# A fused attention and mixer kernel: the weight conversion's shift as a ScalarE copy, softmax sums inverted by groups of query tiles

## The chip, the cores and the metric

The kernel runs on one core of a Trainium2 chip. The metric is the device time of one execution in microseconds. Three runs of the kernel before took 928.18, 929.75 and 927.37 us; their median is 928.18. In what follows PE is TensorE, DVE is VectorE, ACT is ScalarE, POOL is GpSimd and SP is SyncE. PEld is PE's weight load, and a name with a q at its end is an engine's own queue or sequencer.

## The reference, cut to what matters

Three stages run in a row, for 4 batches of 576 tokens. Attention has 8 heads of 64 columns, is causal and has a bias from a running sum of `s`; a gated feed-forward part (512 to 1024 to 512) and a token and channel mixer (256 and 1536 wide) follow. The part that the change touches in the first stage is the softmax:

```python
scores = np.where(causal, -1000000000.0, scores + np.minimum(bias, 0.0))
scores = scores - np.max(scores, axis=-1, keepdims=True)
attn = np.exp(scores)
attn = attn / (np.sum(attn, axis=-1, keepdims=True) + 1e-09)
return np.matmul(attn, v).astype(np.float32)
```

The weights of the two later stages arrive as float64: they are drawn as float32 and multiplied by a float64 scalar.

## The kernel before, in words

**Tiles and stages.** A head's 576 query rows are cut into five tiles j = 0 to 4 of 128 rows, the last of 64. Causality leaves tile j the first 128 j + 128 (or 576) keys. Tiles 0 and 1 make up a head's first chunk (256 columns, `QC`), tiles 2 to 4 its second (320, `CM`). Batch 0 is done in float32: `early` (L300) does tiles 0 and 1 of its 8 heads, `late` (L346) tiles 2 to 4. Batches 1 to 3 are 24 visits, one for each head, with operands split into a high and a low part: `scores` (L265), `transposes` (L387) and `values` (L425).

**One query tile.** PE writes the scores to PSUM. DVE adds the mask, writes the negated scores to the SBUF tile P and keeps the row's extremum (`softmax_max`, L247). `softmax` (L256) then has ACT take the exponential in place, with the row sum as a second output (L260), DVE add 1e-9 (L261) and invert (L262), and POOL multiply P by the inverse (L263). PE transposes P by 128 columns (L314, L365 or L397), ACT copies the transposed tile from PSUM (for batches 1 to 3 with the difference to it from DVE, L422 and L423), and PE multiplies it with the values (L324, L383, L445). P has one buffer for each j (in `early` two), the transposed tile has two PSUM banks.

**Weights.** They come in 85 pieces. `weight_load` (L537) brings a piece as pairs of 32-bit words, and `weight_split` (L546) makes float32 of them: ACT multiplies the high words (L549), DVE shifts the low words right by 29 bits in place (L550), DVE joins three bits and the rest of the high words (L551), then the sign (L552); for one matrix ACT halves the result (L554). ACT writes the high part (L555), and POOL, or DVE for that matrix, the low part (L556). 12 pieces are 512 words wide, 69 are 256 and 4 are 288. The first 12 (`w_k`, `w_r`) and the 16 of `w_v` are converted beside batch 0's attention, the others (`w_tok1`, `w_ch1`, `w_tok2`, `w_ch2`) after attention has ended, beside the feed-forward part of the last batch and the start of the mixer. Raw pieces use 5 buffers at first, later 6.

**The order of the work.** The program is unrolled. Each instruction belongs to one engine, and each engine works in the order of its own queue. That order is made when the program is built: a planner plays the program through with its own costs for each instruction and takes, among those whose inputs it holds ready, the one of highest priority. `at(place)` (L67) sets the priority. Attention items stand at places 16 + n, three to a head for batch 0, five for a visit; feed-forward units of a batch stand behind the items that they are to run beside, so that PE has products between the steps of softmax. `attention_item` (L580) emits an item, with the loads and splits of later heads. `place` (L234) issues four transfers and `load` (L203) one, all on SP's queue, where the weights' loads are issued too.

**What depends on what around the change.** A tile's transposes need its P normalised. P's buffer comes free for the next head after the transposes. The feed-forward part needs on POOL the low part of the squares (L475, tile KK), in the same queue as the normalisations and the weights' low parts.

Of the kernel before, what the change touches and what calls it, by code (L numbers as in the profile page):

```python
# [8 lines left out]
F32 = mybir.dt.float32  # L9
F32R = mybir.dt.float32r  # L10
BF16 = mybir.dt.bfloat16
I32 = mybir.dt.int32
AF = mybir.ActivationFunctionType
ALU = mybir.AluOpType
# [9 lines left out]
def attention_moe_mixer(  # L24
# [16 lines left out]
    nc = tc.nc  # L41
    G, D, _, S = qk.shape
# [10 lines left out]
    NS = (S + 127) // 128  # L53
    QC = 256
# [3 lines left out]
    scale = 1.0 / float(D) ** 0.5  # L58
# [21 lines left out]
    const = ctx.enter_context(tc.tile_pool(name="const", bufs=1, reuse_waits="tile"))  # L80
# [5 lines left out]
    ident = const.tile([128, 128], F32, name="ident")  # L86
# [36 lines left out]

    # P^T of the first chunk: key block 0, then what causality leaves of key block 1. Of the
    # second chunk: key block k at BLK[k], the last in columns that its neighbour leaves unused.
    FIRST = QC + 128
    BLK = [CM * k for k in range(NS - 1)] + [CM * (NS - 2) - (128 * (NS - 1) - QC)]
    ft, pt = {}, {}

    # Tiles that batch 0 uses in float32 and the rest as float32r parts.  # L130
    def x_tile(slot, dtype=F32):
        return qk_p.tile([128, 2 * S], dtype, tag=f"X{slot}", name=f"X{slot}").rearrange("p (t s) -> p t s", t=2)

    def pt_tile(slot, dtype=F32):
        return pt_p.tile([128, (NS - 1) * CM], dtype, tag=f"PT{slot}", name=f"PT{slot}")
# [20 lines left out]

    # Rows (1, -8 cum_q) and (8 cum_k, 1) whose products add the bias, in float32 for the
    # first chunk of batch 0 and as hi and lo for the rest.
    def bias_rows(cp):
# [34 lines left out]

    # A visit is a head and the query tiles it covers. Per pair of heads HL holds
    # (q_lo, q_hi, k_lo, k_hi); per head X1 holds (q, k) as [bias rows; zeros; hi] and
    # X2 holds [q_lo; q_hi] and [k_hi; k_lo].
    HLv = HL.rearrange("p (t s) -> p t s", t=4)
# [48 lines left out]
    def softmax_max(j, ps, P, mx, x, c0, c1):  # L247
# [6 lines left out]
        )  # L254

    def softmax(j, P, mx, x):  # L256
        m = min(128, S - 128 * j)
        w = 128 * j + m
        sm = st_p.tile([128, 2], F32, tag="sum", name="sum")
        nc.scalar.activation(out=P[0:m, 0:w], in_=P[0:m, 0:w], func=AF.Exp, bias=mx[0:m, x:x + 1], scale=-1.0, accum_out=sm[0:m, 0:1])  # L260
        nc.vector.tensor_scalar(out=sm[0:m, 0:1], in0=sm[0:m, 0:1], scalar1=1e-9, scalar2=1.0, op0=ALU.add, op1=ALU.mult)  # L261
        nc.vector.reciprocal(out=sm[0:m, 1:2], in_=sm[0:m, 0:1])  # L262
        nc.gpsimd.tensor_scalar(out=P[0:m, 0:w], in0=P[0:m, 0:w], scalar1=sm[0:m, 1:2], scalar2=1.0, op0=ALU.mult, op1=ALU.mult)  # L263

# [15 lines left out]

    # Batch 0's first chunk, in float32 throughout: HL holds (q, k) of four heads, two more
    # tiles of two each.
    early_at = [(HL, 0, 4)]
# [16 lines left out]
    def early(h, j, V0, cp):  # L300
# [8 lines left out]
        if j == 0:  # L309
            pt[0] = ps_t.tile([128, 512], F32, tag="t", name="t")  # L310
        ps = pt[0]
        for k in range(j + 1):
            o = 128 * (j + k)
            nc.tensor.transpose(ps[:, o:o + 128], P[:, 128 * k:128 * k + 128], ident)  # L314
        if j == 0:
            return
        T = cp.tile([128, FIRST], F32, tag="T", name="T", bufs=2)
        copy("A", T, ps[:, 0:FIRST])
# [10 lines left out]

    # Batch 0's second chunk, in float32 too.  # L330
    late_x, late_v, late_t, late_ps = {}, {}, {}, {}
# [14 lines left out]
    def late(h, j):  # L346
        m = min(128, S - 128 * j)
        w = 128 * j + m
        q0 = 128 * j
# [8 lines left out]
        softmax(j, P, mx, y)  # L358
        if j == QC // 128:
            late_t[h] = pt_tile(h % 2)  # L360
        T = late_t[h]
        pt = ps_t.tile([128, 512], F32, tag="t", name="t")
# [115 lines left out]

    # sigmoid(z) = (tanh(z / 2) + 1) / 2; the half is in w_v.
    def gate(b, c, m):  # L480
# [62 lines left out]

    # float64 words to float32 bits (scaled by 2 ** -half), then to two 12-bit parts: 2 ** -112
    # on the high word, read as a float32, is the change of exponent bias.
    def weight_split(key, hi, lo, half=0):  # L546
        t = raw.pop(key)
        low, high = t[:, :, :, 0], t[:, :, :, 1]
        copy("A", f32(high), f32(high), 2.0 ** -112)  # L549
        nc.vector.tensor_scalar(out=low, in0=low, scalar1=29, scalar2=None, op0=ALU.logical_shift_right)  # L550
        nc.vector.scalar_tensor_tensor(out=low, in0=high, scalar=3, in1=low, op0=ALU.logical_shift_left, op1=ALU.bitwise_or)  # L551
        nc.vector.scalar_tensor_tensor(out=low, in0=high, scalar=-2 ** 31, in1=low, op0=ALU.bitwise_and, op1=ALU.bitwise_or)  # L552
        if half:
            copy("A", f32(low), f32(low), 0.5)  # L554
        copy("A", hi, f32(low))  # L555
        (nc.vector if half else nc.gpsimd).tensor_tensor(out=lo, in0=f32(low), in1=f32(hi), op=ALU.subtract)  # L556
# [23 lines left out]
    def attention_item(n):  # L580
# [48 lines left out]
        with at(N0 + n):  # L629
            scores(i, j)  # L630
            transposes(i, j)
        with at(N0 + n + 0.3):
# [132 lines left out]

    # The low part of the last rows of YN lies below their high part, to meet the high part
    # of w_tok1 (in both halves) in one pass with it.
    def y_transpose(b, h):
# [151 lines left out]
```

## Time and profile before

The profiled execution has a span of 925.0 us from its first to its last instruction. The page gives the span alone, so no other time of that execution is known; it lies 3.2 us under the median of the three runs.

| | us of busy time | share of the span | instructions |
|---|---|---|---|
| PE | 877.3 | 95% | 6032 |
| PEld | 801.9 | 87% | 6032 |
| DVE | 542.4 | 59% | 1667 |
| ACT | 444.4 | 48% | 1211 |
| POOL | 297.6 | 32% | 405 |
| span of the profiled execution | 925.0 | | 17127 |
| median of three runs | 928.18 | | |

Busy time is the union of an engine's instructions, waiting left out. Matmuls are pipelined, so a busy PE is not a PE at its peak. The shares are means over stages that differ: up to some 75 us batch 0's attention and the first weights, up to 450 us attention and feed-forward together, up to 600 us the rest of the feed-forward part with the mixer's weights, then the mixer alone.

### The profile page before, as it was taken

The page shows a single profiled execution, that of the slowest core. Times are in us where ns is not written, and L with a number is a line of the kernel's source. Part 1 is how long each engine was busy: PE and PEld are TensorE (multiplying, and loading weights), DVE is VectorE, ACT ScalarE, POOL GpSimd, SP SyncE. Part 2 cuts the span into 40 slices and gives each one's busy share as a digit, 9 for nine tenths or more (in the row PEclk, how much of TensorE's full clock was granted, in tenths as well). Part 3 has the DMA queues.
Part 4 walks back from the last instruction along what each step waited for, and adds up shares of the span by engine and source line. Part 5 has one row for each costly group of instructions (what it writes and reads, how often), then busy time and mean ns, then how long its engine had stood idle before and what let it go on. Part 6 is the DMA issues. An engine that isn't in the chain of part 4 may idle for free.

```text
span 925.0 us, 17127 instructions
## 1 busy us (share of the span) xinstructions
PE 877.3 (95%) x6032; PEld 801.9 (87%) x6032; DVE 542.4 (59%) x1667; ACT 444.4 (48%) x1211; POOL 297.6 (32%) x405
## 2 busy tenths in 40 slices
PE   6869999999899999899999688999999999999998
PEld 4427678998799999899999578999999999999998
DVE  6897776677798567886479967632223222322220
ACT  4667757767777756668376645321112111311120
POOL 5673446644665625554154644200000000000000
PEclk9988999999899999899999899999999999999999
DMA  7952445455643535442125543500010001000000
GB/s 180 267 130 73 121 92 129 108 134 136 143 97 97 116 82 132 94 110 40 52 83 161 160 141 119 181 7 15 15 44 12 15 16 43 12 9 22 18 6 29
DMA packets 57222, 79.61 MB, mean 86 GB/s; under 512 B 6144, under 2 KB 36096, under 8 KB 57136
## 3 DMA queue, kind: packets, MB, share of 16 engines
q1 hardware_dynamic: 55264, 77.92, 32.4%
q8 instruction: 48, 0.79, 0.3%
q10 hardware_dynamic: 1872, 0.59, 0.3%
q14 instruction: 38, 0.31, 0.1%
HBM read 46.67 MB, written 10.03 MB: 61 GB/s over the span
## 4 chain that ended last, share of the span: by engine, by line
PE 71%; DVE 10%; DMA 8%; issue 5%; ACT 3%; POOL 2%; SPq 0%; ACTq 0%; POOLq 0%; DVEq 0%
PE c L107 32%; PE vd L107 7%; PE h L107 7%; PE t L107 4%; PE pv L445 4%; PE r L107 4%; PE t L397 3%; DMA X<-HL 2%; PE s L275 2%; PE s L276 2%; DVE raw L552 2%; PE pv L383 2%; DVE raw L551 1%; DMA raw<-in_moe_w_ch_dram 1%; DVE t L461 1%
## 5 line engine op out<-in xcount | busy, mean ns | idle before, releaser
L107 PE MATMUL c<-XR,C 128*128 128x320 f32 (+1 forms) x1152 | 158.6, 298 | 2.9 <-DVE KK L780 2.1
L107 PEld LDWEIGHTS c<-XR,C 128*128 128x128 f32 x1152 | 155.2, 190 | 4.2 <-DVE KK L780 3.1
L263 POOL TENSOR_SCALAR P<-P,sum 64x576 f32<-64x576 f32 (+4 forms) x160 | 107.4, 675 | 118.1 <-DVE sum L262 56.1
L107 PE MATMUL vd<-KK,WV 128*128 128x256 f32 (+1 forms) x768 | 124.6, 304 | 5.2 <-POOL KK L475 4.9
L107 PE MATMUL h<-XK,WK 128*128 128x256 f32 (+1 forms) x768 | 123.4, 306 | 5.2 <-ACT XK L462 3.6
L107 PEld LDWEIGHTS h<-XK,WK 128*128 128x128 f32 x768 | 109.6, 195 | 9.5 <-ACT XK L462 5.3
L107 PEld LDWEIGHTS vd<-KK,WV 128*128 128x128 f32 x768 | 108.0, 192 | 10.0 <-POOL KK L475 6.1
L260 ACT ACTIVATE P<-P,mx 64x576 f32<-64x576 f32 (+4 forms) x160 | 95.9, 600 | 33.0 <-DVE mx L250 29.3
L107 PE MATMUL c<-KK,WV 128*128 128x256 f32 (+1 forms) x768 | 106.4, 294 | 0.0
L107 PEld LDWEIGHTS c<-KK,WV 128*128 128x128 f32 x768 | 103.0, 188 | 0.0
L779 ACT ACTIVATE KK<-c 128x256 fp32r<-128x256 f32 (+1 forms) x64 | 26.1, 411 | 146.0 <-PE c L107 146.0
L250 DVE CUSTOM_DVE_ANT_0 P<-s,maskc 64x288 f32<-64x288 f32 (+4 forms) x160 | 75.0, 473 | 22.7 <-PE s L276 8.6
L821 DVE TENSOR_TENSOR u<-c,u 128x256 f32<-128x256 f32 (+1 forms) x32 | 14.7, 458 | 123.2 <-PE c L107 123.2
L74 ACT ACTIVATE raw<-raw 128x256 f32<-128x256 f32 (+2 forms) x101 | 46.7, 468 | 43.6 <-DMA raw<-in_moe_w_ch_dram 18.4
L780 DVE SCALAR_TENSOR_TENSOR KK<-c,KK 128x256 fp32r<-128x256 f32 (+1 forms) x64 | 29.1, 456 | 65.5 <-ACT KK L779 65.5
L107 PE MATMUL r<-XR,WR 128*128 128x320 f32 (+1 forms) x384 | 65.6, 306 | 1.4 <-DVE WK L775 1.4
L475 POOL TENSOR_TENSOR KK<-k,KK 128x256 fp32r<-128x256 f32 (+1 forms) x64 | 54.9, 861 | 28.1 <-ACT k L474 27.0
L107 PEld LDWEIGHTS r<-XR,WR 128*128 128x128 f32 x384 | 55.3, 193 | 3.1 <-DVE WK L775 1.6
L107 PE MATMUL c<-XK,WR 128*128 128x320 f32 (+1 forms) x384 | 55.8, 294 | 0.0
L397 PE MATMUL t<-ident,P 128*128 128x128 f32 (+1 forms) x360 | 53.7, 266 | 2.0 <-DVE sum L261 1.1
L107 PEld LDWEIGHTS c<-XK,WR 128*128 128x128 f32 x384 | 52.4, 188 | 0.0
L423 DVE TENSOR_TENSOR PT<-t,PT 128x384 fp32r<-128x384 f32 (+1 forms) x96 | 44.1, 465 | 13.1 <-ACT PT L422 11.7
(109 smaller groups left out, 1521.0 us busy)
## 6 DMA issues: line engine op xcount, KB each, us to landing
X<-HL SPq DMA_DIRECT2D x72, 288.0 KB
raw<-in_moe_w_ch_dram SPq DMA_DIRECT2D x48, 256.0 KB
HL<-in_qk_dram SPq DMA_DIRECT2D x12, 576.0 KB
yt<-y_d SPq DMA_DIRECT2D x16, 288.0 KB
raw<-in_moe_w_k_dram SPq DMA_DIRECT2D x8, 512.0 KB
raw<-in_moe_w_v_dram SPq DMA_DIRECT2D x16, 256.0 KB
VS<-in_v_dram SPq DMA_DIRECT2D x12, 256.0 KB
y_d<-e SPq DMA_DIRECT2D x16, 160.0 KB
```

The source lines that it names most:

```text
L74: nc.scalar.activation(out=out, in_=in_, func=AF.Copy, scale=scale)
L107: nc.tensor.matmul(ps, a, b, start=first and i == 0, stop=last and i == n - 1)
L250: nc.vector.tensor_tensor_reduce(out=P[0:m, c0:c1], in0=ps[0:m, 0:c1 - c0], in1=maskc[0:m, 512 - q0 + c0:512 - q0 + c1], scale=-scale, sca ...
L260: nc.scalar.activation(out=P[0:m, 0:w], in_=P[0:m, 0:w], func=AF.Exp, bias=mx[0:m, x:x + 1], scale=-1.0, accum_out=sm[0:m, 0:1])
L263: nc.gpsimd.tensor_scalar(out=P[0:m, 0:w], in0=P[0:m, 0:w], scalar1=sm[0:m, 1:2], scalar2=1.0, op0=ALU.mult, op1=ALU.mult)
L275: nc.tensor.matmul(ps[0:m, 0:c1 - c0], x1[:, 0, q0:q0 + m], x1[:, 1, c0:c1], start=True, stop=False)
L397: nc.tensor.transpose(ps[0:r, p0 + m * k:p0 + m * k + m], P[0:m, 128 * k:128 * k + r], ident[0:m, 0:m])
L423: nc.vector.tensor_tensor(out=view(PT[1]), in0=pv, in1=f32(view(PT[0])), op=ALU.subtract)
L445: nc.tensor.matmul(ps[:, o:n], vv[0:r, k, :], pair[t], start=(k == 0 and t == 0), stop=(k == nk - 1 and t == 1),)
L475: nc.gpsimd.tensor_tensor(out=kk[:, 1, m, 0:n], in0=t[:, 0:n], in1=f32(kk[:, 0, m, 0:n]), op=ALU.subtract)
L779: nc.scalar.activation(out=hi, in_=ps, func=AF.Relu)
L780: nc.vector.scalar_tensor_tensor(out=lo, in0=ps, scalar=0.0, in1=f32(hi), op0=ALU.max, op1=ALU.subtract)
```

## The change

In `weight_split` the shift of the low words on DVE becomes an ACT instruction, a copy that reads them as unsigned integers, multiplies by slightly less than 2 to the -29, adds -0.496 and writes unsigned integers. In `softmax` the addition, the inversion and the multiplication by the inverse are taken out; the row sums of a group of query tiles go to neighbouring columns of one small tile (four such tiles, filled with 1 at the start and used in turn). `normalize` does one addition and one inversion for the group and one multiplication for each of its tiles. A group is a head's first chunk (tiles 0 and 1) or its second (tiles 2 to 4). All transposes of a group come after its `normalize`; `late`'s become a function of their own. Comments were taken out as well.

```diff
+    sums = []
+    for x in range(4):
+        t = const.tile([128, 2, NS - QC // 128], F32, name=f"sums{x}")
+        nc.gpsimd.memset(t, 1.0)
+        sums.append(t)
+    open_rows = []
+
     def softmax(j, P, mx, x):
         m = min(128, S - 128 * j)
         w = 128 * j + m
-        sm = st_p.tile([128, 2], F32, tag="sum", name="sum")
-        nc.scalar.activation(out=P[0:m, 0:w], in_=P[0:m, 0:w], func=AF.Exp, bias=mx[0:m, x:x + 1], scale=-1.0, accum_out=sm[0:m, 0:1])
-        nc.vector.tensor_scalar(out=sm[0:m, 0:1], in0=sm[0:m, 0:1], scalar1=1e-9, scalar2=1.0, op0=ALU.add, op1=ALU.mult)
-        nc.vector.reciprocal(out=sm[0:m, 1:2], in_=sm[0:m, 0:1])
-        nc.gpsimd.tensor_scalar(out=P[0:m, 0:w], in0=P[0:m, 0:w], scalar1=sm[0:m, 1:2], scalar2=1.0, op0=ALU.mult, op1=ALU.mult)
+        sm = sums[0]
+        y = len(open_rows)
+        nc.scalar.activation(out=P[0:m, 0:w], in_=P[0:m, 0:w], func=AF.Exp, bias=mx[0:m, x:x + 1], scale=-1.0, accum_out=sm[0:m, 0, y:y + 1])
+        open_rows.append((P, m, w))
+
+    def normalize():
+        sm = sums.pop(0)
+        n = len(open_rows)
+        nc.vector.tensor_scalar(out=sm[:, 0, 0:n], in0=sm[:, 0, 0:n], scalar1=1e-9, scalar2=1.0, op0=ALU.add, op1=ALU.mult)
+        nc.vector.reciprocal(out=sm[:, 1, 0:n], in_=sm[:, 0, 0:n])
+        for y, (P, m, w) in enumerate(open_rows):
+            nc.gpsimd.tensor_scalar(out=P[0:m, 0:w], in0=P[0:m, 0:w], scalar1=sm[0:m, 1, y:y + 1], scalar2=1.0, op0=ALU.mult, op1=ALU.mult)
+        open_rows.clear()
+        sums.append(sm)
...
         softmax(j, P, mx, 0)
         if j == 0:
-            pt[0] = ps_t.tile([128, 512], F32, tag="t", name="t")
-        ps = pt[0]
-        for k in range(j + 1):
-            o = 128 * (j + k)
-            nc.tensor.transpose(ps[:, o:o + 128], P[:, 128 * k:128 * k + 128], ident)
-        if j == 0:
             return
+        rows = [r[0] for r in open_rows]
+        normalize()
+        ps = ps_t.tile([128, 512], F32, tag="t", name="t")
+        for y, R in enumerate(rows):
+            for k in range(y + 1):
+                o = 128 * (y + k)
+                nc.tensor.transpose(ps[:, o:o + 128], R[:, 128 * k:128 * k + 128], ident)
...
         softmax(j, P, mx, y)
-        if j == QC // 128:
+        if j == NS - 1:
+            rows = [r[0] for r in open_rows]
+            normalize()
             late_t[h] = pt_tile(h % 2)
+            for y, R in enumerate(rows):
+                late_transpose(h, QC // 128 + y, R)
+
+    def late_transpose(h, j, P):
+        m = min(128, S - 128 * j)
+        q0 = 128 * j
         T = late_t[h]
...
+    TOP3 = 2.0 ** -29 * (1.0 - 2.0 ** -11)
+
     def weight_split(key, hi, lo, half=0):
         t = raw.pop(key)
         low, high = t[:, :, :, 0], t[:, :, :, 1]
         copy("A", f32(high), f32(high), 2.0 ** -112)
-        nc.vector.tensor_scalar(out=low, in0=low, scalar1=29, scalar2=None, op0=ALU.logical_shift_right)
+        nc.scalar.activation(out=low.bitcast(U32), in_=low.bitcast(U32), func=AF.Copy, scale=TOP3, bias=-0.496)
...
             scores(i, j)
-            transposes(i, j)
+            if j in (QC // 128 - 1, NS - 1):
+                normalize()
+                for y in range(0 if j < QC // 128 else QC // 128, j + 1):
+                    transposes(i, y)
```

## Rows read from the trace of the kernel before

**Rows 1.** Stretches: busy us (count) by engine, granted clock, DMA share, GB/s.

```profile
0.00:50.00 50.00, 40.62 (x110) 22.75 (x111) 37.86 (x137) 29.56 (x76) 29.70 (x53) 1.00 0.91 230
50.00:70.00 20.00, 11.25 (x34) 4.36 (x32) 19.46 (x45) 11.93 (x28) 14.34 (x14) 0.77 0.40 91
...
130.00:450.00 320.00, 309.37 (x2183) 284.81 (x2182) 237.09 (x866) 221.53 (x615) 164.05 (x238) 0.98 0.46 106
...
485.00:530.00 45.00, 37.58 (x248) 35.77 (x247) 43.59 (x89) 29.14 (x81) 25.44 (x29) 0.92 0.51 155
530.00:600.00 70.00, 63.48 (x469) 60.90 (x470) 49.74 (x133) 32.39 (x89) 26.86 (x28) 0.95 0.48 150
600.00:925.00 325.00, 321.69 (x2384) 317.51 (x2381) 86.75 (x202) 58.33 (x150) 0.00 (x0) 1.00 0.06 19
```

**Rows 2.** L550: as a group of one shape, then its shortest, median and longest.

```profile
L550 DVE TENSOR_SCALAR raw<-raw 128x256 int32<-128x256 int32 x69 | 26.2, 381 | 19.0 <-DMA raw<-in_moe_w_ch_dram 9.4 <-DMA raw<-in_moe_w_v_dram 5.8 <-DMA raw<-in_moe_w_tok_dram 1.4
...
L550 DVE TENSOR_SCALAR raw<-raw x85: 269/295/1087, 14.2 to 588.8; 128x256 int32<-128x256 int32 x69, 128x512 int32<-128x512 int32 x12, 128x288 int32<-128x288 int32 x4
```

**Rows 3.** DVE's busy us (count) by L550 alone, in the same stretches.

```profile
0.00:50.00 50.00, 5.50 (x11) 1.00 0.91 230
50.00:70.00 20.00, 2.42 (x5) 0.77 0.40 91
...
485.00:530.00 45.00, 10.10 (x22) 0.92 0.51 155
530.00:600.00 70.00, 9.62 (x28) 0.95 0.48 150
```

**Rows 4.** 485 to 530 us: waits (us, times, longest), then a group of POOL.

```profile
POOL C L556 <- ACT C L74: 12.4, 10, 4.5
ACT C L74 <- DVE raw L552: 10.5, 11, 1.5
...
PE vd L107 <- POOL KK L475: 4.9, 3, 2.1
...
L556 POOL TENSOR_TENSOR C<-raw,C 128x256 fp32r<-128x256 f32 x21 | 18.2, 875 | 18.6 <-ACT C L74 12.4 <-DMA y_d<-e 6.2
```

**Rows 5.** Waits of 50 to 70 us.

```profile
PE s L356 <- DVE mx L250: 4.7, 4, 2.3
```

**Rows 6.** ACT's copies of raw words (count, busy us, mean ns, idle us before).

```profile
L74 ACT ACTIVATE raw<-raw 128x256 f32<-128x256 f32 x85 | 36.8, 438 | 37.6 <-DMA raw<-in_moe_w_ch_dram 18.4 <-DMA raw<-in_moe_w_v_dram 9.0 <-DMA raw<-in_moe_w_tok_dram 6.7
...
L74 ACT ACTIVATE raw<-raw 128x512 f32<-128x512 f32 x12 | 8.1, 673 | 4.2 <-DMA raw<-in_moe_w_k_dram 2.1 <-DMA raw<-in_moe_w_r_dram 2.1
```

**Rows 7.** An inversion, an addition; additions' busy us (count) in 50 to 70.

```profile
L262 DVE RECIPROCAL sum<-sum 128x1 f32<-128x1 f32 x128 | 19.6, 155 | 1.8
...
L261 DVE TENSOR_SCALAR sum<-sum 128x1 f32<-128x1 f32 x128 | 18.3, 145 | 21.4 <-ACT P L260 20.7
...
50.00:70.00 20.00, 0.68 (x5) 0.77 0.40 91
```

**Rows 8.** POOL's fills of small tiles.

```profile
L183 POOL MEMSET e<- 32x192 f32 x12 | 2.7, 267 | 7.5 <-DMA ext_d<-e 7.5
```

**Rows 9.** POOL's normalisation of tiles 3, 4 and 2.

```profile
L263 POOL TENSOR_SCALAR P<-P,sum 128x512 f32<-128x512 f32 x32 | 27.5, 858 | 26.0 <-DVE sum L262 14.0 <-ACT PF L406 3.8 <-ACT PT L422 3.0
...
L263 POOL TENSOR_SCALAR P<-P,sum 64x576 f32<-64x576 f32 x32 | 25.4, 793 | 45.1 <-DVE sum L262 21.9 <-ACT PT L422 6.2 <-ACT PF L406 4.4
...
L263 POOL TENSOR_SCALAR P<-P,sum 128x384 f32<-128x384 f32 x32 | 22.3, 696 | 23.9 <-DVE sum L262 9.3 <-PE t L397 4.9 <-DVE sum L261 2.3
```

**Rows 10.** The longest exponential and the longest maximum.

```profile
L260 ACT ACTIVATE P<-P,mx 64x576 f32<-64x576 f32 x32 | 24.7, 773 | 9.8 <-DVE mx L250 7.8 <-DVE sum L262 1.1 <-POOL P L263 0.5
...
L250 DVE CUSTOM_DVE_ANT_0 P<-s,maskc 128x512 f32<-128x512 f32 x32 | 21.8, 682 | 2.1 <-PE t L365 0.6 <-PE s L276 0.6 <-POOL P L263 0.4
```

**Rows 11.** Second-chunk scores of batch 0: shortest/median/longest ns, first and last start.

```profile
L356 PE MATMUL s<-X x64: 406/488/1062, 35.2 to 131.6; 68*64 68x288 f32 x32, 68*128 68x384 f32 x16, 68*128 68x512 f32 x16
```

**Rows 12.** PE's transposes of batches 1 to 3.

```profile
L397 PE MATMUL t<-ident,P 128*128 128x128 f32 (+1 forms) x360 | 53.7, 266 | 2.0 <-DVE sum L261 1.1
```

More of the change, by code (lines that the diff above doesn't have):

```diff
@@ L12 @@
 I32 = mybir.dt.int32
+U32 = mybir.dt.uint32
 AF = mybir.ActivationFunctionType
```

## The prediction

> **What bounds the kernel now.** I read the busy time by stage first. One stretch after another shows which engine is full [rows 1]. From 600 us on, TensorE (PE) works 321.69 of 325 us, VectorE (DVE) 86.75 and ScalarE (ACT) 58.33: nothing the change touches can move that part except by letting it begin earlier. From 130 to 450 us, the attention of batches 1 to 3, PE works 309.37 of 320 us and DVE 237.09. Two stretches look different. In 50 to 70 us DVE works 19.46 of 20 us and PE 11.25, at a granted clock of 0.77, a mean over its two levels, 1.2 and 2.4 GHz. In 485 to 530 us DVE works 43.59 of 45 us and PE 37.58, at 0.92. There DVE is the limit, and PE loses 8.75 and 7.42 us by idle time alone. Before 50 us the limit is partly the DMA engines, at 0.91 of their time, with DVE at 37.86 of 50.
>
> The groups of instructions then show what DVE does in these two stretches: the weights. Each piece of float64 weights takes three DVE instructions (L550 to L552), and the shift L550 takes 381 ns on 256 columns, from 269 to 1087 [rows 2]. By stage it takes 5.50 us before 50, 2.42 in 50 to 70, 10.10 in 485 to 530 and 9.62 in 530 to 600 [rows 3]. The waits of 485 to 530 show how that reaches PE: ACT waits 10.5 us for DVE's raw words, POOL 12.4 us for ACT's high part, and behind those low parts in POOL's queue stands the square's low part (KK, L475), for which PE waits 4.9 us [rows 4]. In 50 to 70 PE waits 4.7 us for DVE's maxima, which free the score banks [rows 5].
>
> **The change, part by part.** *The shift leaves DVE.* 85 instructions go: 69, 12 and 4 by width. DVE loses 5.50, 2.42, 10.10 and 9.62 us in the stages above; the few left over lie where PE is full, at no gain. *ACT gets 85 copies instead.* The trace has no ACT instruction on integers. Its nearest rows are ACT's copies of the neighbouring words, with the same stride and width: 438 ns on 256 columns, 673 on 512 [rows 6]. I take these, since only the type differs. I bound it from below by L550's own quickest run, 269 ns [rows 2], and from above by POOL's 875 ns for the low part of such a piece [rows 4].
>
> In 485 to 530 us 22 shifts go: DVE falls from 43.59 to 33.5 us. ACT rises from 29.14 by 22 x 0.438 = 9.6 to 38.8 us; with the bounds it is 35.1 to 48.4. PE needs 37.58. The fullest engine is then ACT at 38.8, so the stretch could lose up to 45 - 38.8 = 6.2 us. I take half, 3.1, because each piece now passes ACT twice before its first DVE join, and ACT's queue also holds the activations that PE and POOL wait for. In 530 to 600 PE is idle 6.5 us and DVE loses 9.62 of 49.74 us, but some of that idle time is load latency; I take 1.5 us.
>
> In 50 to 70 us five shifts go, 2.42 us; ACT rises from 11.93 by 5 x 0.673 = 3.4 us at most to 15.3, still under 20. Before 50, 5.50 us go from DVE, but with DMA at 0.91 I count none of it by itself; what is left over from there as a backlog is my upper bound.
>
> *The sums are inverted by group.* Before: 160 additions and 160 reciprocals, 145 and 155 ns [rows 7]. After: one pair for each head's first chunk (tiles 0 and 1) and for each second chunk (tiles 2 to 4): 8 + 8 + 24 x 2 = 64. DVE loses 96 x 0.30 = 29 us, and a part of the 21.4 us for which it stands before L261 on full tiles, waiting for the exponential [rows 7]. Most of it lies in 130 to 450, where PE covers it: I credit nothing there. In 50 to 70 there are five pairs [rows 7], 1.5 us; two thirds go, 1.0 us. So that stretch loses 2.42 + 1.0 = 3.4 us of a queue that is 97% full; I take 3.0, since the rest is ACT's and POOL's.
>
> *What is added with it.* Four fills of small tiles on POOL, 267 ns each by the nearest row [rows 8], 1.1 us at the start if the mask stands behind them; POOL is busy 29.70 of the first 50 us [rows 1], so I take 0 and keep the 1.1 for the range. And the wait: POOL's normalisation of tiles 2 and 3 is held until tile 4 has its exponential, then three run in a row, 696 + 858 + 793 = 2.35 us [rows 9]. The last tile is ready 1.55 us later than now. Queued behind these on POOL are KK's low parts and the splits of the next heads; behind them wait PE's transposes, then the value products. Tiles 2 to 4 have one buffer each, so the next head's maximum of tile 2 waits for these transposes as well. In batch 0's second chunk, where no tile 0 or 1 lies between heads, one head's loop through its own buffers is at most four maxima at 0.68, the last exponential 0.77, the pair 0.30 and the first normalisation 0.70, 4.5 us with no hand-overs [rows 7, 9, 10]. A head takes (131.6 - 35.2) / 8 = 12 us there now, from first score to last [rows 11], so it fits even at twice that. In 130 to 450 a head takes 320 / 24 = 13 us and two tiles lie between: 0 as well, covered by PE's waiting products of the MoE part. PE's transposes there wait little now, 2.0 us over all 360 [rows 12].
>
> Sum: 3.0 + 3.1 + 1.5 = 7.6 us off the profiled span of 925.0, or 917.4. The span is 3.2 us under the median of the three runs, 928.18, which I take as what lies around it: **920.5 us**.
>
> One rule speaks against the first part. The Trainium skill (ScalarE: Activation LUTs, Rules for kernel authors) puts multiplications and additions on VectorE rather than ScalarE. Per instruction this trace agrees, 438 ns against 381 [rows 2, 6]: by that rule alone the 69 pieces of 256 columns would cost 69 x 0.057 = 3.9 us of engine time more and the sum would hold no gain from them.
>
> **The rivals.** *ACT becomes the limit in 485 to 530.* If an integer copy costs over (45 - 29.14) / 22 = 0.72 us, ACT is full for all 45 us; at POOL's 875 ns it holds 48.4, 3.4 us more than the stretch has now; with 4.5 us less from the other stretches that is 928.18 + 3.4 - 4.5 = 927.1, no change. For it: ACT's queue is in order, and 10.5 us of its time there are already waits. Against: its copies of the same words take 0.438. This is where the rule of the Trainium skill (ScalarE: Activation LUTs) would lead.
>
> *The late normalisation reaches PE.* Each of the 32 second chunks puts 1.55 us between softmax and the transposes. PE's queue is in order; its order is fixed when the program is built, from a planner's own costs and not from the durations of this trace. If PE stands for it in 10 of 32, that is 15.5 us, net +8: 936. In all 24 later heads it would be 37. It decides against the gain from 5 groups on (7.6 / 1.55). For it: PE is full there, so what it stands idle is not won back, and before each of the three shapes POOL already stands 24 to 45 us in all [rows 9]. Against: the 2.0 us above.
>
> *DVE's backlog before 50 us counts too.* If early conversions, not DMA, hold up the buffers, 5.50 us and half of the 16 pairs of the first chunks, 2.4, come on top: 928.18 - 7.6 - 7.9 = 912.7.
>
> **How the numbers follow.** A measurement tells about 0.3%, 2.8 us, from no change. The forecast (914 to 925) has 0.47; the backlog case 0.10; ACT as the limit, or gains too small to tell, 0.16, within 2.8 us of before; the late normalisation 0.27, slower. So faster 0.57, same 0.16, slower 0.27. The forecast's own range is 914 to 925. To hold 8 in 10, the range goes from 909, below the backlog case, to 936, the price of 10 groups; what lies outside is the far end of the late normalisation and larger gains.
>
> **What the next profile would show.** Right: L550 gone from DVE, 85 ACT copies at 0.43 to 0.47 us on 256 columns; 64 additions and 64 reciprocals; DVE under 40 us in the stretch of the channel weights, which ends 3 us or more sooner; PE's first MoE product, now behind 50 to 70 us, some 3 us sooner; the last stage unchanged in length. Wrong: ACT over 95% busy there; idle time before PE's transposes (t from P) in tens of us instead of two; a longer stretch between the first score of batch 1 and the last one. A change of PE's idle time at the loads of q and k, which nothing here touches, would mean that the new order of the queues alone moved the time.

## The result, and the profile after

The changed kernel takes 937.91 us (median of 7 runs, 934.47 to 942.26), the kernel before 928.18 in the same comparison: a ratio of 1.010, with a 95% interval from 1.0069 to 1.0131. It is slower by 1.0%, and 1.9 us above the range. The profiled execution's span went from 925.0 to 932.9 us.

I cut both spans at three marks that the timeline gives: the first score of batch 1, the first score of its thirteenth visit (a visit is a head of batches 1 to 3), and the last score. The busy time by stretch, in the columns of [rows 1], of the kernel before:

```profile
133.80:271.10 137.30, 130.82 (x905) 117.66 (x902) 101.71 (x389) 97.60 (x277) 78.41 (x111) 0.98 0.53 123
271.10:446.40 175.30, 171.15 (x1231) 160.75 (x1230) 130.23 (x463) 120.43 (x331) 83.27 (x122) 0.98 0.41 95
446.40:925.00 478.60, 461.12 (x3397) 451.91 (x3395) 203.07 (x474) 140.86 (x375) 66.49 (x74) 0.99 0.18 56
```

The same stretches of the changed kernel, with the two of [rows 1] that the forecast hung on (50 to 70, and the 45 us of the channel weights, now at 499 to 544), and one of 10 us:

```profile
50.00:70.00 20.00, 10.69 (x32) 4.62 (x31) 19.26 (x35) 15.52 (x35) 12.19 (x9) 0.68 0.28 90
...
139.20:293.10 153.90, 136.60 (x897) 119.27 (x895) 106.47 (x327) 97.31 (x278) 82.12 (x115) 0.96 0.48 109
293.10:463.20 170.10, 163.52 (x1176) 152.70 (x1177) 123.11 (x373) 117.52 (x330) 83.83 (x118) 1.00 0.42 97
463.20:932.90 469.70, 457.68 (x3410) 448.81 (x3408) 191.22 (x421) 155.66 (x432) 63.99 (x76) 0.99 0.18 57
499.00:544.00 45.00, 39.58 (x277) 37.19 (x276) 39.04 (x72) 37.25 (x112) 25.75 (x29) 1.00 0.49 145
...
150.00:160.00 10.00, 5.59 (x22) 4.92 (x23) 5.86 (x12) 4.34 (x13) 9.39 (x12) 0.66 0.53 116
```

Two things happened at once. The stretch after the last score, with the weights of the mixer in it, is 8.9 us shorter (478.6 to 469.7). The first twelve visits are 16.6 us longer (137.3 to 153.9), and PE is idle in them for 17.3 us instead of 6.5. The other 5.8 us are PE's longer busy time, for 8 instructions fewer, at a granted clock of 0.96 against 0.98. In 150 to 160 us alone PE is idle 4.4 us, and the granted clock of these 10 us is 0.66, a mean over the two levels of 1.2 and 2.4 GHz. Batch 1 also begins 5.4 us later, and the last twelve visits take 5.2 us less: +5.4 + 16.6 - 5.2 - 8.9 = +7.9.

The groups of instructions that answer to [rows 2, 6, 7, 9] (busy us, mean ns, idle us before and what ended it):

```profile
L581 ACT ACTIVATE raw<-raw 128x256 uint32<-128x256 uint32 x69 | 30.0, 435 | 0.0
...
L280 POOL TENSOR_SCALAR P<-P,sums 128x384 f32<-128x384 f32 x32 | 24.1, 752 | 90.9 <-DVE sums L278 64.0 <-ACT P L271 11.6 <-ACT KK L501 7.1
...
L277 DVE TENSOR_SCALAR sums<-sums 128x3 f32<-128x3 f32 x32 | 9.5, 296 | 7.3 <-ACT P L271 7.1
...
L581 ACT ACTIVATE raw<-raw 128x512 uint32<-128x512 uint32 x12 | 8.0, 664 | 0.0
...
L278 DVE RECIPROCAL sums<-sums 128x3 f32<-128x3 f32 x32 | 5.5, 171 | 0.7
```

and the additions by their line, durations as shortest, median and longest:

```profile
L277 DVE TENSOR_SCALAR sums<-sums x64: 136/169/1951, 10.5 to 465.0; 128x2 f32<-128x2 f32 x32, 128x3 f32<-128x3 f32 x32
```

ACT's integer copies cost what the float copies cost (435 and 664 ns against 438 and 673 [rows 6]). POOL now stands 90.9 us ahead of tile 2's normalisation, 23.9 before [rows 9], since that tile waits for the whole group. The waits of the first twelve visits (us, times, longest), the changed kernel first, then the counterparts in the kernel before:

```profile
POOL P L280 <- DVE sums L278: 22.1, 7, 6.6
...
DVE P L251 <- PE t L425: 8.6, 9, 4.7
PEld h L108 <- DVE XK L491: 5.8, 3, 3.1
...
PE h L108 <- DVE XK L491: 5.1, 3, 2.8
```

```profile
POOL P L263 <- DVE sum L262: 9.4, 10, 1.9
...
PE h L107 <- ACT XK L462: 1.2, 2, 1.0
```

The visit with the changed kernel's longest waits for t and XK shows how that reaches PE (start us, length us, engine, line, idle before it):

```profile
148.87 0.76 ACT L271 ACTIVATE P<-P,mx 64x576 f32<-64x576 f32 x1
...
149.81 2.96 POOL L233 TENSOR_TENSOR VV<-VS,VV 128x512 fp32r<-128x512 f32 x2
...
152.39 1.95 DVE L277 TENSOR_SCALAR sums<-sums 128x3 f32<-128x3 f32 x1
...
152.74 1.53 POOL L221 TENSOR_TENSOR HL<-HL 128x288 f32<-128x288 f32 x2
...
154.38 0.18 DVE L278 RECIPROCAL sums<-sums 128x3 f32<-128x3 f32 x1
...
154.73 0.47 DVE L491 TENSOR_TENSOR XK<-t,XK 128x320 fp32r<-128x320 f32 x1
154.73 3.42 POOL L280 TENSOR_SCALAR P<-P,sums 128x384 f32<-128x384 f32 x5 [0.41 <-DVE sums L277]
...
155.25 4.89 PE L108 MATMUL h<-XK,WK 128*128 128x320 f32 x16 [2.85 <-DVE XK L491]
...
159.97 0.49 PE L425 MATMUL t<-ident,P 128*128 128x128 f32 x3
...
160.61 0.56 DVE L251 CUSTOM_DVE_ANT_0 P<-s,maskc 128x384 f32<-128x384 f32 x1 [4.69 <-PE t L425]
```

Tile 4's exponential ends at 149.6. DVE's queue reaches the group's addition only at 152.4, and the addition lasts 1.95 us beside POOL's two-input instructions, where its median is 0.17. Behind it in DVE's queue stands the join of XK, for which PE waits 2.85 us. POOL can begin the normalisations only at 154.7, five in a row; the transposes come at 160.0, behind a block of 16 products; and DVE stands 4.7 us for the tile's buffer. The row of 150 to 160 above is this place.

### The profile page after: what moved, and what is told of

Read it like the earlier page. It is cut to its first block, busy times and chain, and to the rows that moved or that the text cites. A ratio compares the mean times of both kernels' runs of the same rounds, so it can differ in the third digit from the quotient of the medians.

```text
span 932.9 us, 16857 instructions
## 1 busy us (share of the span) xinstructions
PE 875.2 (94%) x6032; PEld 798.4 (86%) x6032; DVE 521.0 (56%) x1390; ACT 466.2 (50%) x1296; POOL 293.9 (32%) x409
## 4 chain that ended last, share of the span: by engine, by line
PE 66%; DMA 12%; DVE 8%; ACT 6%; issue 5%; POOL 2%; SPq 1%; ACTq 0%; POOLq 0%; DVEq 0%
PE c L108 33%; PE h L108 6%; PE vd L108 6%; PE t L108 5%; DMA X<-HL 4%; DMA HL<-in_qk_dram 3%; PE r L108 3%; PE pv L473 3%; PE t L425 2%; DMA ext_d<-e 2%; PE pv L411 2%; PE s L376 2%; PE s L294 1%; PE s L295 1%; DVE t L489 1%
## 5 line engine op out<-in xcount | busy, mean ns | idle before, releaser
L108 PE MATMUL c<-XR,C 128*128 128x320 f32 (+1 forms) x1152 | 155.9, 295 | 0.0
L108 PEld LDWEIGHTS c<-XR,C 128*128 128x128 f32 x1152 | 153.0, 188 | 0.8 <-DVE KK L814 0.8
L108 PE MATMUL h<-XK,WK 128*128 128x256 f32 (+1 forms) x768 | 128.0, 308 | 14.1 <-ACT XK L490 6.3
L280 POOL TENSOR_SCALAR P<-P,sums 64x576 f32<-64x576 f32 (+4 forms) x160 | 101.2, 648 | 111.3 <-DVE sums L278 75.1
L108 PEld LDWEIGHTS vd<-KK,WV 128*128 128x128 f32 x768 | 105.9, 188 | 8.8 <-POOL KK L503 2.9
L855 DVE TENSOR_TENSOR u<-c,u 128x256 f32<-128x256 f32 (+1 forms) x32 | 14.6, 457 | 119.9 <-PE c L108 119.9
L582 DVE SCALAR_TENSOR_TENSOR raw<-raw 128x256 int32<-128x256 int32 (+2 forms) x85 | 49.7, 586 | 30.3 <-ACT raw L581 26.8
L583 DVE SCALAR_TENSOR_TENSOR raw<-raw 128x256 int32<-128x256 int32 (+2 forms) x85 | 56.0, 660 | 1.2
```

The costliest lines, as they stand in the source:

```text
L108: nc.tensor.matmul(ps, a, b, start=first and i == 0, stop=last and i == n - 1)
```

## The experiments

**The parts alone.** Theory A was that the grouped, later normalisation loses the time and the shift gains; B, that ACT's copies lose it; C, that only the order of the queues, which the planner makes anew for each variant, moved. The first run puts the shift on ACT and leaves the sums as they were.

```diff
-        nc.vector.tensor_scalar(out=low, in0=low, scalar1=29, scalar2=None, op0=ALU.logical_shift_right)
+        nc.scalar.activation(out=low.bitcast(U32), in_=low.bitcast(U32), func=AF.Copy, scale=TOP3, bias=-0.496)
```

> Kernel before with the shift alone moved to ScalarE; every softmax tile is inverted and normalised alone, as before. Theory A (the grouped, later normalisation loses the time between 145 and 250 us, and the moved shift is worth what its two stretches gain): 920 to 925 us, with the first score of batch 1's second visit near 148 us as before and no lag of 10 us or more at 250 us. Theory B (the ScalarE copies lose the time, as ScalarE's queue holds up the rest): 933 us or more. Theory C (the new order of all queues moves the time, whatever the edit): anywhere from 920 to 938, with the stalls at other places.

Measured: 912.47 us, ratio 0.9861 (0.9827 to 0.9895), 7.5 us under the lowest of what A, B and C expected. Its stretches:

```profile
129.60:263.60 134.00, 126.81 (x870) 112.24 (x869) 101.06 (x383) 95.59 (x272) 77.50 (x112) 1.00 0.55 125
263.60:439.70 176.10, 171.85 (x1267) 162.45 (x1266) 136.94 (x469) 121.35 (x340) 86.75 (x123) 1.00 0.41 95
439.70:910.20 470.50, 460.03 (x3397) 451.79 (x3395) 190.54 (x419) 155.42 (x430) 62.68 (x74) 0.99 0.18 57
```

Against before, batch 1 begins 4.2 us sooner, the visits take 2.5 us less and the end 8.1 us less; PE's idle time in the first twelve visits stays at 7.2 us. The second run groups the sums and leaves the shift on DVE (the diff of `softmax` and `normalize` without that of `weight_split`).

> Kernel before with the groups alone; the shift stays on VectorE. Theory A: 938 to 946 us, 10 us or more behind the kernel before at 250 us, and VectorE's maxima wait for PE's transposes two or three times as long as the 3.9 us between 130 and 450 us before. Theory B: 925 to 930. Theory C: anywhere from 920 to 940.

Measured: 943.02 us, ratio 1.0189 (1.0156 to 1.0221). That is as A has it. B falls: the loss is the grouping's. The third is the changed kernel with only tiles 0 and 1 in a group:

```diff
-            if j in (QC // 128 - 1, NS - 1):
+            if j != 0:
                 normalize()
-                for y in range(0 if j < QC // 128 else QC // 128, j + 1):
+                for y in range(0 if j < QC // 128 else j, j + 1):
                     transposes(i, y)
```

> The changed kernel, but only tiles 0 and 1 of a head form a group; tiles 2, 3 and 4 are each inverted, normalised and transposed as soon as their exponential is done. Theory A, and if it is the second chunk that holds the buffers: 918 to 927 us, and VectorE's waits for PE's transposes back to some 4 us. If any grouping does it: 934 or more. Theory C: anywhere.

Measured: 913.19 us, ratio 0.9859 (0.9834 to 0.9885), 5 us under A's band and the same as the shift alone. The pairs of the first chunk cost and bring nothing that can be told; the loss is the second chunk's group of three.

**Is it the single buffers?** My first form of theory A was that the group holds the single buffers of tiles 2 and 3. I gave them two.

```diff
-        P = p_p.tile([128, w], F32, tag=f"P{j}", name=f"P{j}")
+        P = p_p.tile([128, w], F32, tag=f"P{j}", name=f"P{j}", bufs=2 if j in (2, 3) else 1)
```

> The changed kernel with two buffers each for the score tiles 2 and 3 (tile 4 keeps one, for want of space). If the single buffers carry the loss, the next head's maxima no longer wait for the transposes: 922 to 930 us and VectorE's waits for transposes under 3 us. If it is the later transposes themselves that PE misses, 934 to 940. Theory C: anywhere.

Measured: 925.74 us, ratio 0.9983 (0.9965 to 1.0001), 12 us back, a time as the single buffers would have it. But DVE's waits for the tiles' transposes, expected under 3 us, are 15.0 between 130 and 480 us, and the first twelve visits take hardly less than 153.9:

```profile
136.70:289.60 152.90, 136.86 (x905) 120.65 (x905) 104.71 (x331) 101.73 (x285) 83.35 (x120) 0.96 0.49 112
```

What came back lies before and behind them. The same edit on the shift alone (there with five buffers for the sums instead of six), and on the kernel with pairs:

> The kernel before with the shift on ScalarE and, besides, two buffers for the softmax tiles P2 and P3 of the second chunk; every sum is inverted alone, as before. Theory A (the grouping holds P2 and P3 until the group's end, and what that holds up is DVE's queue of maxima, the score banks and the transfers X<-HL): without grouping a P tile is released soon after its own normalisation, so second buffers have little to give: 905 to 914 us, against 912.5 for the shift alone. The rival (single P buffers were costly in the kernel before as well, and the grouping only added to it): the second buffers give back nearly as much here as the 12 us they gave the changed kernel, 898 to 903 us.

> The changed kernel with only the first two query tiles inverted together, each tile of the second chunk alone, and two buffers for P2 and P3. Theory A: the loss was of the second chunk's group, and with it gone the second buffers have little to give: 905 to 914 us, against 913.2 without them. The rival (single P buffers cost time whatever is grouped): 898 to 904 us.

Measured: 914.33 us, ratio 0.9864 (0.9822 to 0.9906), and 907.23 us, ratio 0.9802 (0.9768 to 0.9837). Both are as theory A has them, the first 0.3 us above its band: the buffers bring nothing there, or some 5 us (0.9859 to 0.9802). The next run was meant to hold the buffers as long as the changed kernel does, but without a late inversion: each tile of the second chunk is inverted and normalised alone, and in the program's text its transposes stand behind the last tile's normalisation.

```diff
-        if j == NS - 1:
-            rows = [r[0] for r in open_rows]
-            normalize()
+        normalize()
+        late_P[j] = P
+        if j == NS - 1:
+            for y in range(QC // 128, NS):
+                late_transpose(h, y, late_P.pop(y))
```

(and the same in `attention_item`).

> The changed kernel, but each tile of the second chunk is inverted and normalised as soon as its sum is there, and only its transposes (and with them the release of P2, P3 and P4) wait for the end of the group. Theory A, in the form that the held buffers and the transposes in one block carry the loss: 930 to 940 us, as the changed kernel's 937.9. Its rival, that the late normalisation on GpSimd (a burst of three tiles at the group's end, 2.2 us in a row) carries the loss: 911 to 917 us, as the kernel with pairs alone (913.2). A time between, 920 to 928, says that both do.

Measured: 907.99 us, ratio 0.9818 (0.9785 to 0.9852), 3 us under the rival's band. But the trace shows that nothing was held. In the first twelve visits tile 2's first transpose starts on average 1.8 us after the end of the head's last exponential, as in the shift alone (1.8) and nearly as in the kernel before (1.4); in the changed kernel it is 4.9. So the run says nothing on held buffers. It is the kernel with pairs in another order, and what the changed kernel adds to it is that tiles 2 and 3 are normalised only after tile 4's exponential, with the later transposes and the later release of the buffers that follow from it. That this late normalisation costs the time I call theory D; that held transposes alone would cost nothing, as some expectations below say, is not shown. Its stretches:

```profile
134.50:271.90 137.40, 131.24 (x903) 118.51 (x902) 99.95 (x364) 97.72 (x276) 77.34 (x111) 0.98 0.52 120
271.90:440.60 168.70, 167.41 (x1218) 157.22 (x1217) 126.50 (x430) 118.94 (x329) 85.39 (x121) 1.00 0.42 98
440.60:903.70 463.10, 453.40 (x3401) 445.26 (x3399) 192.12 (x421) 155.86 (x430) 62.41 (x74) 1.00 0.18 58
```

**Smaller groups, and lateness without a group.** From the held transposes: tile 2 alone with 3 and 4 grouped, then 2 and 3 grouped with 4 alone.

```diff
-        normalize()
+        if j != NS - 2:
+            normalize()
```

(in the second run `j != QC // 128`.)

> As the run with held transposes (908.0 us), but only the sum of tile 2 is inverted at once; tiles 3 and 4 are inverted together, so that tile 3's normalisation on GpSimd (0.86 us) comes behind tile 4's exponential. Theory D (the loss is the normalisations that stand between a head's last exponential and its transposes; the held transposes alone cost nothing): one of the two late normalisations is back, so about half of the 30 us: 917 to 928 us. Theory C (the order that the planner draws makes the time, whatever is late): no relation to the number of late tiles; within 8 us of 908 as likely as above 930.

> As the run with held transposes (908.0 us), but tiles 2 and 3 are inverted together and tile 4 alone: the group ends one tile before the head's end, and nothing but tile 4's own normalisation stands behind the last exponential. Theory D: 905 to 915 us, the same as without this group. Theory C: anywhere from 900 to 935.

Measured: 916.84 us, ratio 0.9890 (0.9868 to 0.9911), 0.2 us under what D expects; and 925.02 us, ratio 0.9998 (0.9968 to 1.0027), which it doesn't: a group that ends a tile sooner costs 17 us. The first twelve visits take 146.1 and 147.3 us, with 10.5 and 11.4 us of idle PE. Lateness behind the last exponential alone is too narrow, or the order has a share. Then the reverse: every sum of the second chunk alone, but tile 4 multiplied by one twice more on POOL.

```diff
+            for z in range(2 if w == S else 0):
+                nc.gpsimd.tensor_scalar(out=P[0:m, 0:w], in0=P[0:m, 0:w], scalar1=sm[0:m, 1, 2:3], scalar2=1.0, op0=ALU.mult, op1=ALU.mult)
```

> The run with held transposes (908.0 us), every sum inverted alone, but tile 4 is multiplied by one twice more on GpSimd after its normalisation: 2 x 0.79 = 1.6 us more between a head's last exponential and the tile's transposes, as long as the group's two late normalisations. Theory D (lateness behind the last exponential costs the time): 918 to 940 us. The rival, that the shared inversion on VectorE's queue costs it: 904 to 913, since only GpSimd gets work, of which it has room (63 of 120 us busy). An order drawn anew may move either by some 8 us.

Measured: 928.80 us, ratio 1.0021 (0.9998 to 1.0044), 21 us above the held transposes. The first twelve visits of that kernel:

```profile
134.80:293.90 159.10, 143.87 (x935) 126.57 (x934) 111.91 (x380) 102.68 (x284) 99.31 (x140) 0.92 0.47 109
```

They are longer than in the changed kernel, with 15.2 us of idle PE. So a loss of this kind needs no group of three and no late tile 2: tile 2's normalisation ends here 3.2 us ahead of the last exponential, where the held transposes have 2.9. The run also gives POOL 51 us of work (32 x 2 x 0.8), which can make later whatever stands behind it in POOL's queue, so it doesn't separate the lateness of tile 4 from the load on POOL, and it was made in one order only.

**The order.** Every variant has another order of the queues. To see what an order is worth, I moved the place of the feed-forward units by half a step in the kernel before, which changes no work.

```diff
-            with at(N0 + n + 3):
+            with at(N0 + n + 2.5):
```

> The kernel before with no work changed; only the due time of the feed-forward units is half a step earlier in the planner, which gives every queue another order (PE 1547 of 5930 instructions stand elsewhere). Theory C (an order drawn anew moves this kernel's time by ten or more microseconds either way, and so the losses and gains seen so far are of that kind): outside 920 to 936 us. Theory A: within 5 us of 927.4, that is 922 to 933.

Measured: 935.14 us, ratio 1.0089 (1.0059 to 1.0119), 8 us for nothing but an order, and between what the two theories expected. Its first twelve visits take 6.6 us more than at the original place, 3, with hardly more idle time of PE (6.7 us for 6.5):

```profile
132.40:276.30 143.90, 137.24 (x908) 121.89 (x907) 105.89 (x400) 100.33 (x283) 78.56 (x113) 0.94 0.54 123
```

So no single pair of runs above proves a cause of under some 10 us. I therefore repeated the whole change, the shift alone and the held transposes at other places (2, 2.5 and 4 for 3).

> The changed kernel with the due time of the feed-forward units half a step earlier, no work changed: another order of the queues for the same late normalisation (PE 1290 of 5930 instructions stand elsewhere). Theory D: the loss stays, 930 to 946 us, the changed kernel's 937.9 with the 9 us that the same edit moved the kernel before. Theory C (the changed kernel only drew a bad order): under 928.

> The run with held transposes, again with the feed-forward units' due time half a step earlier. Theory D: 900 to 918 us, 15 us or more under the changed kernel with the same due time. Theory C: above 920, or within 8 us of the changed kernel with the same due time.

> The changed kernel with the feed-forward units due one step earlier (2 for 3): another order, no work changed. Theory D: 928 to 946 us, 10 to 30 over the shift alone with the same due time. Theory C: within 8 us of the shift alone with the same due time.

> The shift alone with the feed-forward units due one step earlier. Both theories: an order drawn anew, 905 to 928 us; what counts is the difference to the changed kernel with the same due time (theory D 10 to 30 us, theory C within 8).

> The shift alone with the feed-forward units due half a step earlier. The changed kernel took 933.4 us so, the kernel before 935.1. Theory D: 903 to 923 us, at least 10 under the changed kernel. Theory C: 925 or more. The shift's own gain, 15 us at a due time of 3, is tested on a second order as well: if it holds, 920 us.

> The changed kernel with the feed-forward units due one step later (4 for 3). Theory D: 9 to 26 us over the shift alone with the same due time, as in the three orders before. Theory C: within 8 us of it, or under it.

> The shift alone with the feed-forward units due one step later: an order drawn anew, 905 to 928 us. What counts is the difference to the changed kernel with the same due time.

Each cell gives the median, the ratio to the kernel before (place 3) with its interval, and the length of the first twelve visits:

| place | whole change | shift alone | held transposes | group's price |
|---|---|---|---|---|
| 3 | 937.91, 1.0100 (1.0069 to 1.0131), 153.9 | 912.47, 0.9861 (0.9827 to 0.9895), 134.0 | 907.99, 0.9818 (0.9785 to 0.9852), 137.4 | 2.4% |
| 2.5 | 933.44, 1.0088 (1.0053 to 1.0123), 153.5 | 924.17, 0.9972 (0.9947 to 0.9998), 138.3 | 923.36, 0.9967 (0.9939 to 0.9996), 135.0 | 1.2% |
| 2 | 933.84, 1.0088 (1.0055 to 1.0121), 153.6 | 922.05, 0.9955 (0.9925 to 0.9985), 142.0 | | 1.3% |
| 4 | 931.17, 1.0071 (1.0040 to 1.0101), 153.4 | 912.14, 0.9849 (0.9793 to 0.9904), 135.3 | | 2.2% |

The group's price is the whole change's ratio less that of the shift alone: 22, 11, 12 and 21 us of 928. Its sign holds at all four places, and at all four the first twelve visits take 153.4 to 153.9 us, where the shift alone takes 134 to 142. These are not four orders of that stretch, though: there the whole change has the same sequence of instructions on PE, DVE, ACT and POOL (by operation, names and shapes) at places 2, 2.5 and 4, and only place 3 has another, the one that the groups alone have too. With the second buffers that makes three orders with a group of three, at 152.9 to 154.5 us and 14.6 to 17.7 us of idle PE. The kernels without such a group and without the delayed tile 4 or a smaller group in the second chunk have eleven different orders, at 129.7 to 143.9 us and 4.6 to 8.3 us of idle PE. The two kernels at place 4, first twelve visits each, the whole change first:

```profile
138.50:291.90 153.40, 138.25 (x897) 120.60 (x895) 106.06 (x329) 98.93 (x279) 81.92 (x115) 0.94 0.48 111
```

```profile
132.20:267.50 135.30, 129.24 (x867) 116.13 (x866) 100.31 (x380) 96.43 (x271) 77.69 (x112) 0.96 0.54 124
```

PE's idle time is 15.2 us in the one and 6.1 in the other. So an order badly drawn (theory C) falls as the whole cause of the loss. The 30 us between the whole change and the held transposes don't hold as its size either: at place 2.5 they are 10, and an order alone is worth up to 14 us in one kernel (0.9818 to 0.9967). The held transposes at 2.5 came out as C had it, 923.4 us and 10 under the whole change where D wanted 15, and the shift at 2.5 lies 1 us over D's band and 9 under the whole change where D wanted 10. The other five came out as D expects, though the two of the shift alone could hardly have spoken against it by themselves.

## Why the prediction was wrong

**The step that failed** is "0 as well, covered by PE's waiting products of the MoE part", the price of the group's wait. It measured 11 to 22 us at four places. Most of it is in the first twelve visits, 12 to 20 us over the shift alone; 5 to 12 us more arise before batch 1, where the prediction's loop through batch 0's buffers had 0 too, and the last twelve visits give 4 to 15 back. I took the lateness to be that of the last tile, 1.55 us. But in the kernel before, tile 2's normalisation ended on average 5.2, 3.1 and 4.5 us ahead of the end of the head's last exponential (batch 0's 8 heads, the next 12 and the last 12, from the trace's starts and durations); now it ends 2.4, 2.5 and 2.2 us behind it. So tile 2 is 5.6 to 7.6 us later. How much of the loss that makes is not shown: with tile 4 delayed, tile 2 was not late and the visits took longer still. The step that the runs refute is the cover. I took the products of the feed-forward part to cover any delay of a head that still fits into 13 us. In the first twelve visits they don't: a visit takes 12.8 us in both orders of the whole change (153.4 to 153.9 over 12), where it took 11.4 before (12.0 at place 2.5), and PE is idle for 14.6 to 17.3 us of them, 6.5 to 6.7 before. What goes with that in all runs is the end of a head: tile 4's first transpose starts there on average 9.0 to 9.4 us after the last exponential's end wherever three tiles are a group, 9.6 with tile 4 delayed, and 6.8 to 7.7 in every other run. Whether this lag makes the visits long or is made by what makes them long, and which link closes the heads' chain, stays open. Second buffers for tiles 2 and 3 don't shorten it (152.9), so it isn't these alone. Tile 4's buffer, the other buffers and the banks weren't tried one by one.

**The rival had the right sign and nearly the right time, 936, but the wrong place.** It expected PE to stand for POOL's normalisation at its transposes, "idle time before PE's transposes in tens of us". These waits are 1.0 and 1.2 us:

```profile
PE t L425 <- POOL P L280: 1.0, 1, 1.0
...
PE t L393 <- POOL P L280: 1.2, 1, 1.2
```

So its time came near by luck. The other sign of being wrong did show: from the first score of batch 1 to the last one it is 324.0 us, 312.6 before. The idle time lies ahead of other instructions of PE, such as the products that wait for XK, whose join stands in DVE's queue behind the group's addition.

**The shift.** Its copies cost 435 and 664 ns for the 438 and 673 taken, and ACT did not become the limit: 37.25 of 45 us in the channel weights' stretch, forecast 38.8; DVE works 39.04 there, under the 40 named but over the 33.5 worked out. The terms were too small at place 3: the end of the span lost 8.1 us for 4.6 (3.1 + 1.5), the start 4.2 for 3.0, the visits 2.5 for 0, in all 14.8 of the span for 7.6. At this place, half of the 6.2 us that I took off in the weights' stretch was too cautious. But the place matters here too: against the kernel before at place 3, the shift alone gained 1.4, 0.3, 0.5 and 1.5% at places 3, 2.5, 2 and 4, 8 us on average; against the kernel before at the same place it is known twice, 13 us at place 3 and 11 at 2.5. That 50 to 70 us would be unloaded holds for the shift alone, where DVE works 17.08 of 20 us and PE 12.50; in the changed kernel DVE works 19.26. The Trainium skill (ScalarE: Activation LUTs, Rules for kernel authors) puts multiplications and additions on VectorE; per piece the trace agrees (435 ns against 381), for the kernel the runs of the shift alone, 0.3 to 1.5% faster, speak against it, since DVE was the full engine in the weights' stretch.

**The sums.** 64 additions and 64 inversions, as said. DVE saved 18 us by them, not 29: the 64 additions take 19.0 us where 160 took 23.0, and the 64 inversions 10.7 where 160 took 24.6.

**The case of the backlog** (912.7) came out near the shift's 912.5, but by other terms: only 4.2 us of it lie ahead of batch 1.

So the sum was -7.6 + 0 (the span of 917.4 and the 3.2 around it make 920.6, not 920.5), and the runs show -3 to -14 for the shift over four places and +11 to +22 for the group: at place 3, where the change was timed, 1.0% slower.

## What to carry to other kernels

Before work is batched to save instructions, ask for every member of the batch by how much it becomes later, the first as well as the last, follow who waits for each, and don't price the wait at nothing because the busy engine has other work: here it cost more than the batch saved. Where queues are ordered by a planner, any edit draws a new order, and an order alone moved these kernels by 8 to 14 us: repeat a comparison at a few neutral settings before a cause of that size is believed, and see from the traces that the settings did change the order, and that an edit did move what it was meant to move. The two parts of a change are best timed apart: the shift alone was 1.4% faster than before at place 3, and with pairs of the first chunk and single inversions of the second it was 1.8%; at place 2.5 both were 0.3%.

## What the hardware showed unexpectedly

An addition on one column of 128 rows takes 122 to 157 ns whatever POOL does (160 of them before). On two or three columns it takes 160 ns on average with POOL idle (37 of 64), 264 beside one-input instructions of POOL alone (14), but 719 with a two-input instruction of POOL beside it (13), up to 1951 as in the timeline above; the inversions, 147 to 177 ns, show none of this. The Trainium skill (SBUF — State Buffer, Who interferes with whom) has VectorE and GpSimd share a pair of ports that one holds for a whole instruction, and counts VectorE's tensor_scalar among those that can want it; by the Trainium skill (VectorE: DVE Perf Modes, Mode 2×_2P) such a mode splits the outermost dimension longer than one, and a single column has none. The trace agrees with that: one column shows no delay, two and three do. What these 13 additions cost the kernel wasn't tried alone; the run with held transposes has some too, on its pairs, up to 1172 ns, and is the faster one.
